# Opening of a bucket-attention kernel: order of the first head's score passes, key bits, casts and moves

## Chip, cores, metric

The kernel runs on one core of a Trainium2 chip. The metric is device time in microseconds (us), the median of three runs. TensorE multiplies matrices, VectorE and GpSimd do elementwise work and reductions, ScalarE does casts and exponentials, and SyncE (SP) issues most of the transfers, each from its own in-order stream of instructions.

## Reference

Attention over 4 batches of 8 heads, 768 positions and 64 dimensions, in which a query sees only the keys of its own bucket. A bucket is the six signs of a projection. The result goes through a mixture of experts with a capacity for each expert.

```python
q_bits = (np.einsum('bhsd,dk->bhsk', q, proj) > 0)      # k_bits the same
q_bucket = np.sum(q_bits * powers, axis=-1)
mask = q_bucket[:, :, :, None] == k_bucket[:, :, None, :]
scores = np.where(mask, scale * np.matmul(q, k.transpose(0, 1, 3, 2)), -1e9)
attn = np.exp(scores - np.max(scores, axis=-1, keepdims=True))
attn = attn / (np.sum(attn, axis=-1, keepdims=True) + 1e-09)
x = np.matmul(attn, v)                                   # then _moe_ref(x, ...)
```

## The kernel before

The 32 heads are worked off in 8 groups of 4 (two pairs of heads, 128 partitions each). For a group, `load` brings q, k and v in float32; `cast` (L130) makes float16 high parts, `sub` (L132) low parts; `bits` (L144) projects q and k and VectorE turns the result into signs `bt` (L145), which ScalarE scales (`bscale`, L146). `dm`, `dm2` and `moves` then send high parts, low parts and signs to the tiles QA, KA, QB, KB by transfers that SP issues. The signs stand in rows 64 to 69 of QA and KA, so that one matmul gives the score and the bucket match.

A head has six score passes (`S_pass`, L240): two matmuls into one of two PSUM tiles, then a maximum on VectorE (L242). `m_rows` (L248, L249) turns three columns of maxima into a row of QA, by three matmuls and ScalarE. `ST` (L258, L259) computes the transposed scores of 128 keys and 384 queries in two matmuls and ScalarE takes the exponential (L260); it needs the row of maxima of its half. `lo` (L263) takes the low part of the probabilities, on GpSimd or, where the lists E0, E1, PAT say so, on VectorE. `AV` (L273 to L275) multiplies with v. `sumv` (L204, L206) and `sumw` (L210 to L214) prepare a correction row of v's sums, which `AV` needs with its last keys.

The steady loop runs over t, 6 steps for each head. Step t issues `ST(t)` for its first half, the score passes planned for t (of head 2 and later, by S and LEAD), the work of half step 2t, the second half of `ST`, `lo` of step t-1, the work of half step 2t+1 and `AV` of step t-4. Each engine takes its instructions in this order.

Ahead of the loop stands the opening, the string OPS. Its words are issued from left to right: a letter is an operation, a digit its argument; words behind the n-th `|` belong to half step n-1 of the loop. Here b are the signs of head 0 (`tbits`, L223 to L225), t, r and l casts and low parts of heads 0 and 1 from a separate early load `XT` (`first`, L67), s a score pass (s0 to s5 head 0, s6 to s11 head 1), m a row of maxima, e a first half of `ST`, B the `bits` of head 1 (L140, from XT) and of pair 1 (L144), a their scaling, D the transfer of head 1's signs (`bdma`, L317), d and f the moves of pair 1 (L152 to L165), c and u its casts and low parts, v and x those of v, C a copy of constant rows (L319), w matmuls that only keep TensorE busy (L76), g an operation of GpSimd that only waits. Before, heads 0 and 1 are handled by the opening, pair 1 (heads 2 and 3) by c, u, d and f, and group 1's casts are planned at half steps 13 to 23 (list P1). Entries 19 to 21 of P1 are the places of group 1's three loads (L62), entry 18 that of `sumv`.

A tile of group 1 takes the place of that of group 0: the load of q waits for the readers of q of pair 1, and the cast of group 1 (L130) writes the tile that the moves of pair 1 read.

Of the kernel before, what the change touches and what calls it, by code (L numbers as in the profile page):

```python
# [17 lines left out]
DR = bass.MemoryType.DRAM  # L18

AP=dict(PAT=[[0, 5], [3]],  # L20
 E0=[3, 5],
 E1=[3, 4],
 X=[2, 2, 5],
 MR=2,
 LEAD=9,
 S=[7, 30],
 DW=[8, 0, 0, 0, 384],
 P1=[13, 13, 14, 15, 17, 21, 23, 21, 16, 27, 21, 26, 23, 24, 33, 32, 3, 4, 50, -6, 3, 13],
 P2=[41, 44, 48, 49, 51, 51, 57, 55, 45, 49, 55, 57, 52, 60, 59, 60, 2, 3, 74, 32, 36, 47],
 P3=[69, 73, 82, 80, 84, 86, 89, 86, 75, 83, 87, 90, 94, 96, 97, 106, 2, 3, 122, 58, 62, 87],  # L30
 P4=[-33, -33, -25, -21, -13, -7, -11, -7, -20, -16, -5, -2, -7, 5, 8, 10, 2, 4, 38, -56, -51, -11],
 L0=[109, 2],

 EA=[(0,0),(0,0),(307,4)],
 SW=9,
 XL={4:[0,3,5],7:[1,4],8:[0,3,5],10:[0,3,5]},
 BS=2,
 MV=[28, 59, 96, 1],
 CL=9,
 WS=-23,  # L40
 SU=15,
 OPS='b0 i3 i2 t0 w2 b1 w3 r0 r2 s0 w4 C1 r1 t1 c1 s1 B0 c0 a0 D0 w2 w1 s4 w5 s2 s3 r3 v2 w5 v0 g0 l0 l1 C0 m0 s5 w3 s6 r5 w2 l3 e0 e1 d0 u0 u1 s7 v1 l2 w0 m1 e2 | s8 | x0 | w0 | x1 s9 | r4 s10 | | | s11 m2 v3 f0 | x3 | | x2 | m3 | | | | | |')
PAT,E0,E1,DW,LEAD=(AP[k] for k in ('PAT','E0','E1','DW','LEAD'))
NB=dict(S=2,T=3,V=1)
HK=385
EMPTY=60000.0
def attention(tc, nc, ctx, qT, kT, vv, proj, wg, x_dram, L, jp, identf, B, late=None, after=None):
    S=768; NG=2*B; NH=8*B; LAG=4
    cp=ctx.enter_context(tc.tile_pool(name="cp",bufs=1))
    dp=ctx.enter_context(tc.tile_pool(name="dp",bufs=2))  # L50
    psS=ctx.enter_context(tc.tile_pool(name="psS",bufs=NB["S"],space=PS))
    psT=ctx.enter_context(tc.tile_pool(name="psT",bufs=NB["T"],space=PS))
    psV=ctx.enter_context(tc.tile_pool(name="psV",bufs=NB["V"],space=PS))
    V=nc.vector; A=nc.scalar; G_=nc.gpsimd; T=nc.tensor; SY=nc.sync
# [3 lines left out]
    def alloc_load(G):  # L58
        LD[G]=(dp.tile([128,2,S],F32,name="qp",bufs=1),dp.tile([128,2,S],F32,name="kp",bufs=1),dp.tile([128,4,6,64],F32,name="vp",bufs=1))
    def load(G,w):  # L60
        if w==0: alloc_load(G)
        SY.dma_start(LD[G][w],(qT,kT,vv)[w][G])  # L62
    alloc_load(0)
    XT=cp.tile([128,4,6,128],F32,name="XT")
    qd,kd=(XT[:,2*i:2*i+2].rearrange("p d c q -> p d (c q)") for i in range(2))
    def first(j,r):
        for t,src in ((qd,qT),(kd,kT)): SY.dma_start(t[r:r+64,j],src[0][64*j:64*j+64,0])  # L67
    first(0,0); first(0,64); first(1,0)
    for w,src in ((0,qT),(1,kT)): SY.dma_start(LD[0][w][:,1],src[0][:,1])
    SY.dma_start(LD[0][2],vv[0])  # L70
    first(1,64)

    wrm=cp.tile([128,512],F16,name="wrm"); V.memset(wrm,0.0)
    wps=psV.tile([128,512],F32,name="psv")
# [8 lines left out]
    pr=cp.tile([128,32],F32,name="pr"); G_.memset(pr,0.0)  # L83
# [41 lines left out]
    def cast(G,w,p,half=None):  # L125
        if (G,'h') not in TMP:
            TMP[G,'h']=[dp.tile([128,2,S],F16,name=n,bufs=1) for n in ("qh","kh")]
            TMP[G,'l']=[dp.tile([128,2,S],F16,name=n,bufs=1) for n in ("ql","kl")]
        if half is None: A.copy(TMP[G,'h'][w][:,p],LD[G][w][:,p])
        else: A.copy(TMP[G,'h'][w][:,p,half*384:half*384+384],LD[G][w][:,p,half*384:half*384+384])  # L130
    def sub(G,w,p,eng=None):
        (eng or G_).tensor_tensor(TMP[G,'l'][w][:,p],LD[G][w][:,p],TMP[G,'h'][w][:,p],op=ALU.subtract)  # L132
    def bits(G,pairs):
        if (G,'b') not in TMP: TMP[G,'b']=dp.tile([128,S],F16,name="bt",bufs=1)
        bt=TMP[G,'b']; r=slice(0,128)
        ps=psS.tile([128,2,512],F32,name="pss")
        for hf in range(2):
            if G==0:
                for w in range(2):
                    T.matmul(ps[32*w:32*w+32,hf,0:384],pr[0:64],(qd,kd)[w][0:64,1,hf*384:hf*384+384],start=True,stop=True,tile_position=(0,32*w))  # L140
            for p in pairs:
                for w in range(2):
                    cg=64*p+32*w
                    T.matmul(ps[cg:cg+32,hf,0:384],pr,LD[G][w][:,p,hf*384:hf*384+384],start=True,stop=True,tile_position=(0,cg))  # L144
        V.tensor_scalar(bt.rearrange("p (z q) -> p z q",z=2),ps[:,:,0:384],0.0,0.5,op0=ALU.is_gt,op1=ALU.subtract)  # L145
# [89 lines left out]
    def S_pass(h,qc):  # L235
        G,j=divmod(h,4); u=G%2
        if qc==0: M6[h]=dp.tile([128,6],F16,name="m6",bufs=3)
        ps=psS.tile([128,2,512],F32,name="pss")
        for hf in range(2):
            T.matmul(ps[:,hf,0:HK],QA[u][:,j,qc*128:qc*128+128],KA[u][:,j,hf*HK:hf*HK+HK],start=True,stop=True)  # L240
            if h==0: warm(DW[1],DW[4])
        V.tensor_reduce(M6[h][:,qc:qc+1],ps[:,:,0:HK],axis=AX.XY,op=ALU.max,negate=True)  # L242
# [72 lines left out]
    def add(n,f,*a): at.setdefault(n,[]).append((f,a))  # L315
    def bdma():
        for w,a in enumerate((QA,KA)): SY.dma_start(a[0][64:70,1,0:S],TMP[0,'b'][32*w:32*w+6])  # L317
    def copies(a):
        for j in (0,2): SY.dma_start(a[1][64:128,j:j+2,0:S],a[0][64:128,2:4,0:S])  # L319
    OPS=dict(i=lambda j: init(j,A.copy),t=top,b=tbits,r=lambda n: rest(n//3,n%3),l=lambda n: rlo(n//2,n%2),  # L320
        c=lambda w: cast(0,w,1),u=lambda w: sub(0,w,1),s=lambda k: S_pass(k//6,k%6),B=lambda n: bits(0,[1]),D=lambda n: bdma(),
        m=lambda n: m_rows(n//2,n%2),d=lambda n: dm(0,[1]),f=lambda n: dm2(0,[1]),v=lambda j: cv(0,j),x=lambda j: sv(0,j,G_),
        e=lambda k: ST(0,k,0),C=lambda n: copies((QA,KA)[n]),w=lambda n: warm(n,DW[4]),a=lambda n: bscale(0),
        g=lambda n: G_.tensor_copy(tick,KA[0][64:65,0,0:1]))
    n=-1; early=[]
# [6 lines left out]
    for G in range(1,NG):  # L332
        p=AP['P1'] if G==1 else AP['P2'] if G==2 else AP['P3'] if G==3 else [48*(G-1)+x for x in AP['P4']]
        st,sg=(AP['P4'] if G>3 else p)[16:18]
        for w in range(3):
            if G==1 or w==2: add(p[19+w],load,G,w)
        for n in range(8): add(p[n],cast,G,n//2%2,n//4,n%2)
        for n in range(4): add(p[8+n],sub,G,n%2,n//2)
        add(p[12],bits,G,[0,1]); add(p[12]+AP['BS'],bscale,G); add(AP['MV'][G-1] if G<4 else 48*(G-1)+AP['MV'][3],moves,G)
        for j in range(4): add(p[15]+st*j,cv,G,j); add(p[15]+st*j+sg,sv,G,j,G_)  # L340
        add(p[18],sumv,G); add(p[18]+AP['SW'],sumw,G)
        if G>1: add(48*(G-1)+AP['CL'],clear,G)

    k=12; done={}; half={}; S_at={}
# [25 lines left out]
    for t in range(6*NH+LAG+6):  # L370
        h,s=divmod(t,6)
        first=(t-LAG)%6==5
# [585 lines left out]
```

## Time and profile before

| | us |
|---|---|
| runs | 714.18, 717.42, 718.44; median 717.42 |
| profiled execution | 718.04, its span 716.3 |
| TensorE busy in the span | 669.1 (93%) |
| VectorE busy | 516.9 (72%) |
| ScalarE busy | 471.4 (66%) |
| GpSimd busy | 517.1 (72%) |

The profile shows one execution; times in it count from the first instruction. TensorE's matmuls overlap in the pipeline, so a busy TensorE is not at its peak. A row's "idle before" names what released the engine. [...]

### The profile page before, as it was taken

How to read it: one execution, taken by the hardware profiler on the slowest of the kernel's cores; microseconds unless marked ns; L12 is line 12 of the kernel's file. 1: busy time of each engine (PE TensorE's matmuls, PEld its weight loads, DVE VectorE, ACT ScalarE, POOL GpSimd, SP SyncE). 2: the span in 40 equal slices, each digit the busy share in tenths (PEclk: the TensorE clock that was granted, in tenths of full speed). 3: DMA queues.
4: the chain of work that ended last, by engine and by line, in shares of the span. 5: the costliest groups of instructions: out<-in, count | busy, mean ns of one | idle time of the engine just before them, and what ended most of it. 6: DMA issues, size and time to landing. Idle time of an engine off the chain costs nothing. (4 is left out here: it accounts for less than half of the span.)

```text
span 716.3 us, 19197 instructions
## 1 busy us (share of the span) xinstructions
PE 669.1 (93%) x7868; PEld 432.4 (60%) x7868; DVE 516.9 (72%) x1126; ACT 471.4 (66%) x887; POOL 517.1 (72%) x456
## 2 busy tenths in 40 slices
PE   8798999999999999999997679999989999999995
PEld 3466666767767777677766455555545465655552
DVE  6858778888888788788975678778777878734120
ACT  7777887777887778777763045665656565666750
POOL 7769979898988979887663237584857475777761
PEclk9989999999999999999998579999999999999998
DMA  7728672725637256440000160727171727272601
GB/s 199 197 75 207 170 195 76 185 69 137 153 105 193 68 139 151 109 102 24 24 24 25 61 220 14 281 61 263 47 277 44 266 61 264 73 266 81 243 29 45
DMA packets 39952, 93.59 MB, mean 131 GB/s; under 512 B 4548, under 2 KB 30520, under 8 KB 37816
## 3 DMA queue, kind: packets, MB, share of 16 engines
q1 hardware_dynamic: 33048, 46.21, 24.6%
q0 software_dynamic: 6816, 46.15, 18.2%
q8 instruction: 62, 1.02, 0.6%
q14 instruction: 26, 0.21, 0.1%
HBM read 59.53 MB, written 12.58 MB: 101 GB/s over the span
## 5 line engine op out<-in xcount | busy, mean ns | idle before, releaser
L263 POOL TENSOR_TENSOR lo<-pt 128x768 f16<-128x768 f32 x139 | 224.3, 1626 | 47.4 <-ACT pt L260 43.0
L260 ACT ACTIVATE pt<-pst 128x384 f32<-128x384 f32 x384 | 181.2, 492 | 73.3 <-PE pst L259 60.9
L242 DVE TENSOR_REDUCE m<-pss 128x1 f16<-128x770 f32 x192 | 181.1, 956 | 35.8 <-PE pss L240 34.6
L258 PE MATMUL pst<-qa,ka 128*128 128x384 f16 x384 | 125.4, 327 | 2.5 <-ACT qa L249 1.3
L259 PE MATMUL pst<-qb,kb 128*128 128x384 f16 x384 | 125.2, 326 | 1.9 <-DMA qb<-ql 1.9
L275 PE MATMUL psv<-vh,lo 128*128 128x65 f16 x1152 | 121.8, 194 | 1.2 <-POOL lo L263 1.1
L274 PE MATMUL psv<-vl,pt 128*128 128x64 f16 x1152 | 122.1, 193 | 0.0
L273 PE MATMUL psv<-vh,pt 128*128 128x65 f16 x1152 | 122.1, 195 | 0.0
L273 PEld LDWEIGHTS <-pt 128*128 128x128 bf16 x1152 | 107.2, 98 | 11.1 <-issue 3.5
L274 PEld LDWEIGHTS <-pt 128*128 128x128 bf16 x1152 | 106.3, 99 | 8.2 <-issue 0.3
L275 PEld LDWEIGHTS <-lo 128*128 128x128 f16 x1152 | 106.3, 98 | 1.6 <-POOL lo L263 1.6
L785 POOL TENSOR_TENSOR wl<-wf,wh 128x512 f16<-128x512 f32 x76 | 87.2, 1173 | 22.0 <-ACT wf L776 21.6
L240 PE MATMUL pss<-ka,qa 128*128 128x385 f16 x384 | 94.6, 329 | 1.4 <-DVE m L242 0.6
L767 ACT ACTIVATE wh<-wf 128x1024 f16<-128x1024 f32 x64 | 67.0, 1052 | 34.9 <-PE psa L735 20.9
L263 DVE TENSOR_TENSOR lo<-pt 128x768 f16<-128x768 f32 x53 | 73.4, 1385 | 1.6 <-ACT pt L260 1.0
L828 PEld LDWEIGHTS <-wh 128*128 128x128 f16 x512 | 48.3, 98 | 35.5 <-issue 5.4
L840 PEld LDWEIGHTS <-hh 128*128 128x128 f16 x384 | 35.9, 97 | 39.6 <-issue 2.0
L776 ACT ACTIVATE wf<-wf 128x1024 f32<-128x1024 f32 x55 | 58.1, 1057 | 1.0
L831 DVE SCALAR_TENSOR_TENSOR hl<-px,hh 128x384 f16<-128x384 f32 x64 | 34.9, 552 | 31.2 <-ACT hh L830 30.7
L843 ACT ACTIVATE o<-po 128x512 f32<-128x512 f32 x24 | 14.3, 595 | 64.9 <-PE po L840 63.8
L828 PE MATMUL px<-xh,wh 128*128 128x384 f16 x256 | 53.9, 327 | 3.2 <-ACT xh L815 2.4
L240 PEld LDWEIGHTS <-qa 128*128 128x128 f16 x384 | 37.2, 97 | 27.8 <-issue 1.5
(271 smaller groups left out, 1328.0 us busy)
## 6 DMA issues: line engine op xcount, KB each, us to landing
vp<-in_vv_dram SPq DMA_DIRECT2D x8, 768.0 KB
x_dram<-X SPq DMA_DIRECT2D x16, 384.0 KB
qp<-in_qT_dram SPq DMA_DIRECT2D x7, 768.0 KB
kp<-in_kT_dram SPq DMA_DIRECT2D x7, 768.0 KB
qa<-qh SPq DMA_DIRECT2D x14, 192.0 KB
ka<-kh SPq DMA_DIRECT2D x14, 192.0 KB
qb<-qh SPq DMA_DIRECT2D x14, 192.0 KB
kb<-kh SPq DMA_DIRECT2D x14, 192.0 KB
```

What stands on the lines that cost most here:

```text
L240: T.matmul(ps[:,hf,0:HK],QA[u][:,j,qc*128:qc*128+128],KA[u][:,j,hf*HK:hf*HK+HK],start=True,stop=True)
L242: V.tensor_reduce(M6[h][:,qc:qc+1],ps[:,:,0:HK],axis=AX.XY,op=ALU.max,negate=True)
L258: T.matmul(ps[:,0:384],KA[u][:,j,kr],QA[u][:,j,r],start=True,stop=False)
L259: T.matmul(ps[:,0:384],KB[u][:,j,kr],QB[u][:,j,r],start=False,stop=True)
L260: A.activation(PT[h,kc][0][:,r],ps[:,0:384],AF.Exp,scale=0.125)
L263: eng.tensor_tensor(l,p,p.bitcast(BF)[:,1::2],op=ALU.subtract)
L273: T.matmul(av[:,c,:],ph[:,r],VH[u][:,j,kc,:],start=(kc==0 and c==0),stop=False,skip_group_check=True)
L274: T.matmul(av[:,c,0:64],ph[:,r],VL[u][:,j,kc,:],start=False,stop=False,skip_group_check=True)
L275: T.matmul(av[:,c,:],l[:,r],VH[u][:,j,kc,:],start=False,stop=False,skip_group_check=True)
L767: s.nc.scalar.mul(h[:,r],f[:,r],WSC)
L785: for _ in range(n): s.nc.gpsimd.tensor_tensor(*s.pend.pop(0)[1],op=ALU.subtract)
L828: T.matmul(p[:,0:384],a[:,o:o+128],b[:,d],start=n==0,stop=n==11)
```

## The change

The opening is reordered. Head 0's six score passes stand ahead of the bits of head 1 and pair 1 (B0), with three first halves of `ST` (e0 to e2) and the first row of maxima (m0); the score passes of head 1 (s6 to s11) move into the loop, half steps 4 to 11. `C0` moves ahead of `D0`, `f0` from half step 7 to 9. Group 1's loads of q and k (L0, L1) move from half steps -6 and 3 of the planned list into the opening, ahead of the moves d0. `first(1,64)` goes ahead of the loads of pair 1 and of v, and B0 uses all 128 rows of XT and `pr`. The low parts of pair 1 go from GpSimd to VectorE. Head 0's low parts on VectorE are those of steps 0 and 5 instead of 3 and 5, head 1's those of 1, 3 and 4 instead of 3 and 4. S delays the passes of head 2 and a few behind it: the first stands at step 5 instead of 3. `sumv` comes one to three half steps earlier, `sumw` four half steps behind it instead of nine.

```diff
--- before.py
+++ after.py
@@ -18,28 +18,28 @@
 DR = bass.MemoryType.DRAM
 
 AP=dict(PAT=[[0, 5], [3]],
- E0=[3, 5],
- E1=[3, 4],
+ E0=[0, 5],
+ E1=[1, 3, 4],
  X=[2, 2, 5],
  MR=2,
  LEAD=9,
- S=[7, 30],
+ S=[7, 7],
  DW=[8, 0, 0, 0, 384],
- P1=[13, 13, 14, 15, 17, 21, 23, 21, 16, 27, 21, 26, 23, 24, 33, 32, 3, 4, 50, -6, 3, 13],
- P2=[41, 44, 48, 49, 51, 51, 57, 55, 45, 49, 55, 57, 52, 60, 59, 60, 2, 3, 74, 32, 36, 47],
- P3=[69, 73, 82, 80, 84, 86, 89, 86, 75, 83, 87, 90, 94, 96, 97, 106, 2, 3, 122, 58, 62, 87],
- P4=[-33, -33, -25, -21, -13, -7, -11, -7, -20, -16, -5, -2, -7, 5, 8, 10, 2, 4, 38, -56, -51, -11],
+ P1=[13, 13, 14, 15, 17, 21, 23, 21, 16, 27, 21, 26, 23, 24, 33, 32, 3, 4, 49, -6, 3, 13],
+ P2=[41, 44, 48, 49, 51, 51, 57, 55, 45, 49, 55, 57, 52, 60, 59, 60, 2, 3, 72, 32, 36, 47],
+ P3=[69, 73, 82, 80, 84, 86, 89, 86, 75, 83, 87, 90, 94, 96, 97, 106, 2, 3, 121, 58, 62, 87],
+ P4=[-33, -33, -25, -21, -13, -7, -11, -7, -20, -16, -5, -2, -7, 5, 8, 10, 2, 4, 35, -56, -51, -11],
  L0=[109, 2],
 
  EA=[(0,0),(0,0),(307,4)],
- SW=9,
+ SW=4,
  XL={4:[0,3,5],7:[1,4],8:[0,3,5],10:[0,3,5]},
  BS=2,
  MV=[28, 59, 96, 1],
  CL=9,
  WS=-23,
  SU=15,
- OPS='b0 i3 i2 t0 w2 b1 w3 r0 r2 s0 w4 C1 r1 t1 c1 s1 B0 c0 a0 D0 w2 w1 s4 w5 s2 s3 r3 v2 w5 v0 g0 l0 l1 C0 m0 s5 w3 s6 r5 w2 l3 e0 e1 d0 u0 u1 s7 v1 l2 w0 m1 e2 | s8 | x0 | w0 | x1 s9 | r4 s10 | | | s11 m2 v3 f0 | x3 | | x2 | m3 | | | | | |')
+ OPS='b0 i3 i2 t0 w2 b1 w3 r0 r2 s0 w2 s1 C1 C0 r1 t1 w4 s2 r3 w3 s3 r5 g0 l0 l1 m0 s4 e0 s5 e1 e2 l3 B0 c1 m1 c0 a0 D0 u0 u1 L0 L1 l2 v0 e3 d0 | x0 | v1 | x1 | v2 | s6 v3 | x2 s7 | r4 s8 | x3 | s9 | m2 f0 | s10 | s11 | m3 | | |')
 PAT,E0,E1,DW,LEAD=(AP[k] for k in ('PAT','E0','E1','DW','LEAD'))
 NB=dict(S=2,T=3,V=1)
 HK=385
@@ -65,10 +65,9 @@
     qd,kd=(XT[:,2*i:2*i+2].rearrange("p d c q -> p d (c q)") for i in range(2))
     def first(j,r):
         for t,src in ((qd,qT),(kd,kT)): SY.dma_start(t[r:r+64,j],src[0][64*j:64*j+64,0])
-    first(0,0); first(0,64); first(1,0)
+    first(0,0); first(0,64); first(1,0); first(1,64)
     for w,src in ((0,qT),(1,kT)): SY.dma_start(LD[0][w][:,1],src[0][:,1])
     SY.dma_start(LD[0][2],vv[0])
-    first(1,64)
 
     wrm=cp.tile([128,512],F16,name="wrm"); V.memset(wrm,0.0)
     wps=psV.tile([128,512],F32,name="psv")
@@ -137,7 +136,7 @@
         for hf in range(2):
             if G==0:
                 for w in range(2):
-                    T.matmul(ps[32*w:32*w+32,hf,0:384],pr[0:64],(qd,kd)[w][0:64,1,hf*384:hf*384+384],start=True,stop=True,tile_position=(0,32*w))
+                    T.matmul(ps[32*w:32*w+32,hf,0:384],pr,(qd,kd)[w][:,1,hf*384:hf*384+384],start=True,stop=True,tile_position=(0,32*w))
             for p in pairs:
                 for w in range(2):
                     cg=64*p+32*w
@@ -318,7 +317,7 @@
     def copies(a):
         for j in (0,2): SY.dma_start(a[1][64:128,j:j+2,0:S],a[0][64:128,2:4,0:S])
     OPS=dict(i=lambda j: init(j,A.copy),t=top,b=tbits,r=lambda n: rest(n//3,n%3),l=lambda n: rlo(n//2,n%2),
-        c=lambda w: cast(0,w,1),u=lambda w: sub(0,w,1),s=lambda k: S_pass(k//6,k%6),B=lambda n: bits(0,[1]),D=lambda n: bdma(),
+        c=lambda w: cast(0,w,1),L=lambda w: load(1,w),u=lambda w: sub(0,w,1,V),s=lambda k: S_pass(k//6,k%6),B=lambda n: bits(0,[1]),D=lambda n: bdma(),
         m=lambda n: m_rows(n//2,n%2),d=lambda n: dm(0,[1]),f=lambda n: dm2(0,[1]),v=lambda j: cv(0,j),x=lambda j: sv(0,j,G_),
         e=lambda k: ST(0,k,0),C=lambda n: copies((QA,KA)[n]),w=lambda n: warm(n,DW[4]),a=lambda n: bscale(0),
         g=lambda n: G_.tensor_copy(tick,KA[0][64:65,0,0:1]))
@@ -333,7 +332,7 @@
         p=AP['P1'] if G==1 else AP['P2'] if G==2 else AP['P3'] if G==3 else [48*(G-1)+x for x in AP['P4']]
         st,sg=(AP['P4'] if G>3 else p)[16:18]
         for w in range(3):
-            if G==1 or w==2: add(p[19+w],load,G,w)
+            if w==2: add(p[19+w],load,G,w)
         for n in range(8): add(p[n],cast,G,n//2%2,n//4,n%2)
         for n in range(4): add(p[8+n],sub,G,n%2,n//2)
         add(p[12],bits,G,[0,1]); add(p[12]+AP['BS'],bscale,G); add(AP['MV'][G-1] if G<4 else 48*(G-1)+AP['MV'][3],moves,G)
```

## Rows read from the trace of the kernel before

**Rows 1.** Table of stretches: from:to, length, busy us (instructions) by engine, clock, DMA share, GB/s
```profile
22.35:32.90 10.55, 9.64 (x105) 6.13 (x105) 9.81 (x10) 8.22 (x17) 9.71 (x9) 1.00 0.70 206
32.90:36.20 3.30, 0.01 (x2) 0.02 (x2) 2.03 (x2) 1.62 (x4) 3.15 (x3) 0.83 0.87 234
36.20:42.60 6.40, 6.40 (x81) 4.73 (x81) 1.46 (x2) 4.31 (x10) 2.44 (x2) 0.55 0.14 57
65.00:79.00 14.00, 12.14 (x186) 7.89 (x185) 10.71 (x13) 9.52 (x22) 11.80 (x9) 1.00 0.62 177
200.00:240.00 40.00, 39.66 (x638) 28.70 (x637) 33.75 (x45) 31.66 (x69) 35.83 (x39) 1.00 0.47 117
24.90:34.50 9.60, 7.34 (x93) 4.94 (x92) 9.57 (x9) 5.74 (x12) 9.60 (x8) 1.00 0.88 249
```
**Rows 2.** Waits of TensorE, us in total, times, longest: 0:42.6, then 42.6:390
```profile
PE pst L204 <- ACT qa L249: 3.3, 1, 3.3
...
PE pst L259 <- DMA qb<-ql: 1.9, 1, 1.9
```
**Rows 3.** TensorE's timeline in the opening: start us, duration us, operation, [idle before <-releaser]
```profile
11.14 0.83 PE L140 MATMUL pss<-XT,pr 64*32 64x384 f32 x4
...
14.21 0.66 PE L76 MATMUL psv<-wrm 128*128 128x384 f16 x3
...
24.72 0.49 PE L240 MATMUL pss<-ka,qa 128*128 128x385 f16 x2 [0.25 <-DMA ka<-bt]
```
**Rows 4.** TensorE's timeline, one step of the loop at full clock
```profile
26.93 0.19 PE L273 MATMUL psv<-vh,pt 128*128 128x65 f16 x1
...
27.48 0.33 PE L258 MATMUL pst<-qa,ka 128*128 128x384 f16 x1
...
27.80 0.49 PE L240 MATMUL pss<-ka,qa 128*128 128x385 f16 x2
28.14 0.32 PE L258 MATMUL pst<-qa,ka 128*128 128x384 f16 x1
```
**Rows 5.** TensorE's timeline, the bits of group 1: first matmul, and the first behind them
```profile
46.36 0.51 PE L144 MATMUL pss<-qp,pr 128*32 128x384 f32 x1
...
47.79 0.21 PE L273 MATMUL psv<-vh,pt 128*128 128x65 f16 x1
```
**Rows 6.** VectorE's timeline
```profile
10.12 1.94 DVE L242 TENSOR_REDUCE m<-pss 128x1 f16<-128x770 f32 x2 [0.67 <-PE pss L240]
14.35 0.96 DVE L145 TENSOR_SCALAR bt<-pss 128x768 f16<-128x768 f32 x1 [2.29 <-PE pss L144]
...
23.53 4.43 DVE L242 TENSOR_REDUCE m<-pss 128x1 f16<-128x770 f32 x5 [0.71 <-PE pss L240]
27.99 2.23 DVE L263 TENSOR_TENSOR lo<-pt 128x768 f16<-128x768 f32 x1
...
44.49 0.95 DVE L263 TENSOR_TENSOR lo<-pt 128x768 f16<-128x768 f32 x1
```
**Rows 7.** ScalarE's timeline
```profile
15.34 0.84 ACT L146 ACTIVATE bt<-bt 128x768 f16<-128x768 f16 x1 [3.08 <-DVE bt L145]
...
26.11 0.66 ACT L249 ACTIVATE qa<-pst,mbi,msc 32x384 f16<-32x384 f32 x1
...
34.53 0.93 ACT L130 CAST qh<-qp 128x384 f16<-128x384 f32 x2 [3.62 <-DMA kb<-kl]
...
49.92 0.83 ACT L146 ACTIVATE bt<-bt 128x768 f16<-128x768 f16 x1
```
**Rows 8.** SP's timeline of issues: start us, issue us, transfer
```profile
16.21 0.86 SPq L317 DMA_DIRECT2D qa<-bt  x1
17.12 0.72 SPq L317 DMA_DIRECT2D ka<-bt  x1
...
22.68 0.71 SPq L158 DMA_DIRECT2D ka<-bt  x1
...
24.91 0.37 SPq L62 DMA_DIRECT2D qp<-in_qT_dram  x1
```

## The prediction

> **What bounds the kernel now.** I read the table of stretches first, then the waits of TensorE, then the timelines of the five engines over the opening. Between 200 and 240 us TensorE is busy 39.66 of 40 us at full clock [rows 1], and from 42.6 to 390 us it has one wait over 1 us, 1.9 us for the transfer `qb<-ql` before the first transposed score of head 4 [rows 2]. So TensorE sets the pace of the attention. Work that reaches the end of head 0 earlier moves everything behind it, unless a transfer holds it back. [...] The reader should see the cause on ScalarE: the first cast of group 1 (L130) starts at 34.53 us after 3.62 us of waiting, put down to `kb<-kl`, one of the eight moves for heads 2 and 3 [rows 7]. Those moves stand in SP's queue behind the two loads of group 1 issued from 24.91 us [rows 8]. That queue is full: 249 GB/s, DMA share 0.88, from 24.9 to 34.5 us [rows 1]. Everything behind the cast on ScalarE, exponentials and row maxima, waits with it, so TensorE does too.
>
> **What that costs.** 3.3 us idle, and 6.4 us of work at 0.55 that full clock would do in 6.4 x 0.55 = 3.5 us: 2.9 us. Together 6.2 us is what a perfect opening could win back there.
>
> **The change, part by part.** Prices first. Per TensorE step: a transposed pair 27.80 - 27.48 = 0.32 us, a score pass 0.34 us, one `AV` 0.55 us (26.93 to 27.48) [rows 4]. A maximum on VectorE comes every 4.43/5 = 0.89 us [rows 6]. Signs to `bt` 0.96 us [rows 6], scaling on ScalarE 0.84 us, row of maxima 0.66 us [rows 7], a cast of 768 columns 0.8 us (an estimate: just under the scaling, which has as many columns).
>
> (1) *Six score passes ahead of the key bits.* Pass 0 is not moved: its maximum starts at 10.12 us [rows 6]. Six maxima in a row end at 10.12 + 6 x 0.89 = 15.5 us. The third ends at 12.8, so the first row of maxima is written by about 13.9 (0.4 us for the matmuls, 0.66 for ScalarE), and the first transposed score starts near 14.0 us. Three of them and pass 5 take 1.3 us, so the key bits start at 15.3 us instead of 11.14 [rows 3].
>
> (2) *Key bits with 128 rows.* The bits of head 1 used 64 rows of the array, those of pair 1 use 128, and the timeline shows them one after the other: 11.14 to 14.21 us, 3.07 us [rows 3]. Group 1's bits are four column groups of 128 rows, run beside each other, and as many matmuls of as many columns take 47.79 - 46.36 = 1.43 us [rows 5]. With all operands at 128 rows the opening's bits have that same form, so I take 1.43 us; the bounds are 1.43 and 3.07. The bits end at 16.75.
>
> (3) *What then waits.* Signs to 17.8, row of maxima 17.1 to 17.8, cast of q to 18.6, scaling to 19.4. The two transfers of head 1's signs are issued 19.4 and 20.3 (before: 16.21 and 17.12 [rows 8]). From issue to use, the sign transfer issued at 22.68 took until 24.72 [rows 3, 8], 2.0 us. So head 1's first score pass can start at 22.3 us. TensorE has by then only the fourth transposed score and two second halves left, and is done at 18.5. It takes its instructions in order and that pass stands at the third step of the loop, so behind it wait all second halves. **New wait 1: 22.3 - 18.5 = 3.8 us** (3.4 if the transfer takes 1.6).
>
> (4) *Low parts of pair 1 on VectorE.* Alone, a low part takes 0.95 us there, beside a busy GpSimd 2.23 [rows 6]. Without these two, the order gives GpSimd little to do just then, so I take 0.95 each: 18.6 to 20.5, before the signs of head 1 are out, so hidden; at 2.23 the second ends at 23.1 and delays the load of k by about 2 us. The extra low part of head 1 on VectorE costs the same, 0.95 to 2.23, and there VectorE is loaded.
>
> (5) *Loads of group 1 ahead of the moves for heads 2 and 3.* They go out at 21.05 and 21.55, 3.9 us earlier than before. But now the four moves and four sign transfers of pair 1 stand behind them. Two loads of 768 KB and four moves of 96 KB are 1.97 MB; at the 249 GB/s of rows 1 that is 7.9 us: 29.0, with the signs 29.2. Bounds: by issue alone 27.3, at the 234 GB/s of 32.9 to 36.2 us 29.7. Head 2's first score pass stands at step 5 and needs them. From 22.3 TensorE has four score passes paced by maxima, five transposed halves and one `AV`, until 26.5. **New wait 2: 29.2 - 26.5 = 2.7 us** (0.8 to 3.2).
>
> (6) *The old wait.* The eight moves of `dm2` follow those of d0: sixteen transfers at some 0.7 us of issue each [rows 8], from 21.9 us, are issued by 33.1 and the last land near 35, about as before. ScalarE, held by waits 1 and 2, reaches the cast only about then: its own wait is gone or under 1 us. From 29.2 on three maxima (2.7), the row (1.1), `AV` and three passes (1.6) bring TensorE to the sum of v (L204) near 35.1 us, against 36.20.
>
> (7) *From there.* The stretch that took 6.4 us takes 3.5 at full clock; the extra low part on VectorE ahead of the correction of v adds 0.9 to 2.2 (I take 1.3: GpSimd is busy beside it for a part only). 35.1 + 3.5 + 1.3 = 39.9 to 40.7 (with the row of maxima now falling there), against 42.6: 2.4 us ahead, taking 40.2.
>
> (8) *Up to the bits of group 1.* Head 2's passes are two fewer by then, since they start at step 5 instead of 3, so one more maximum (0.89) and what is left of (7) must pass VectorE before the bits: 1.0 us lost. The scaling of group 1's bits (49.92, [rows 7]) comes 1.4 us earlier. All sign transfers, loads and moves of group 1 follow it in SP's order, so the 1.9 us wait of rows 2 moves along, neither shrinking nor growing.
>
> (9) *Sums of v one to three half steps earlier, corrections four instead of nine behind.* Around them TensorE shows no wait in 200 to 240 us [rows 1]: nothing, bounds 0.5 us either way; what covers it is TensorE's own queue.
>
> Sum: -1.4 us against the profiled execution's 718.04 us (span 716.3 and 1.7 around it): 716.6. That execution is 0.6 us above the median of 717.42, so a median would be 716.0. I say 716.4.
>
> **A rule that speaks against it.** After 3.3 us without matmuls the clock stood at 0.55 over the next stretch [rows 1]; after the 1.9 us of rows 2 it did not fall (1.00 from 65 to 79 us, [rows 1]). Wait 1 is of the first kind. [...]
>
> **Rivals.** *Clock falls behind wait 2* (or stays low through it): 2.9 us by the price above, less 0.6 that waits on VectorE cover: 718.7, slower than the profiled execution. It decides when wait 2 is as long as the old 3.3, or when the clock has not risen by 29 us; against it, 2.7 is shorter. *Moves are not held by the loads*: wait 2 shrinks to 0.8, 1.9 gained: 714.5; for it, the bound by issue, against it, the full queue. *The bits are not shortened*: 3.07 us delay everything behind by 1.6: 718.0. *The gain is kept whole*: the 6.2 us and the 1.6 of the bits, off the median: 709.6; against it, the last moves cannot land before 33, so the cast cannot start over 1.5 us earlier. *Several microseconds slower*: a new wait on VectorE at each group, over 725; nothing in rows shows it.
>
> **How the numbers follow.** Forecast 0.56, clock 0.17, moves not held 0.12, bits not shortened 0.06, gain whole 0.05, far slower 0.04. Within 1% is 710.2 to 724.6, about what measurement can tell from no change; only the last two leave it: faster 0.05, same 0.90, slower 0.05. The range goes from the third case, less the 1.7 by which the runs before differ downwards among themselves at the least (717.42 to 714.18 is 3.2), 712.8, to the clock case with 2.23 us low parts, 720.2. The forecast's own range is 714.5 to 718.5.
>
> **What would show it.** Right: key bits of 1.4 us near 15 us; a gap of 3 to 4 us on TensorE before 22 us put down to `ka<-bt`; one of 2 to 3 us before 29; the first cast of group 1 near 35 with little wait; group 1's scaling near 48.5. Wrong: no gap at step 3, or the cast before 33 (faster); or a clock below 1.00 after 30 us (slower).

## The result, and the profile after

The changed kernel takes 720.24 us (median of 13 runs, 716.36 to 722.93), the kernel before, beside it, 715.81 (13 runs, 713.59 to 718.83): ratio 1.0059 (95% interval 1.0035 to 1.0082; intervals stand in square brackets from here on), some 4.4 us slower. 716.4 was forecast, 1 us faster than before. The profiled execution of the changed kernel took 722.02 us (span 720.2), against 718.04.

Lines after the change lie one lower. First the timelines of the profiled execution: start us, duration us, engine, line, operation, [idle before <-releaser]. TensorE to the end of head 0:

```profile
5.05 2.72 PE L222 MATMUL pst<-XT,prt 64*6 64x384 f32 x4 [0.26 <-DMA prt<-in_proj_dram]
...
12.30 0.80 PE L239 MATMUL pss<-ka,qa 128*128 128x385 f16 x2
...
15.47 0.85 PE L239 MATMUL pss<-ka,qa 128*128 128x385 f16 x2
...
16.95 0.49 PE L239 MATMUL pss<-ka,qa 128*128 128x385 f16 x2
...
19.81 0.52 PE L139 MATMUL pss<-XT,pr 128*32 128x384 f32 x2
...
26.77 0.57 PE L239 MATMUL pss<-ka,qa 128*128 128x385 f16 x2 [3.63 <-DMA ka<-bt]
...
34.65 0.82 PE L239 MATMUL pss<-ka,qa 128*128 128x385 f16 x4 [2.39 <-DMA ka<-bt]
```

The two waits of the prediction are there, 3.63 and 2.39 us, both for the signs `ka<-bt` (forecast 3.8 and 2.7). But they end 4.5 and 5.4 us later than forecast, and the first rows show why: the signs of head 0 take 2.72 us for four matmuls, and the first score passes 0.80 to 0.85 us for two, until one at 16.95 takes 0.49. That is TensorE at about half its speed, the lower level, until some 16 us. The granted clock, a share of full speed, reads 1.00 there all the same (from 4.5 to 9.5 us and from 12 to 16), so at the start only the durations tell. In the execution of before that was profiled, the same code up to the first pass ran at the upper level, 1.45 us for the same four matmuls:

```profile
5.18 1.45 PE L223 MATMUL pst<-XT,prt 64*6 64x384 f32 x4 [0.53 <-DMA prt<-in_proj_dram]
...
9.59 0.49 PE L240 MATMUL pss<-ka,qa 128*128 128x385 f16 x2 [0.55 <-DVE ka L225]
```

ScalarE and VectorE:

```profile
39.95 0.92 ACT L129 CAST qh<-qp 128x384 f16<-128x384 f32 x2
...
54.70 0.84 ACT L145 ACTIVATE bt<-bt 128x768 f16<-128x768 f16 x1
...
71.25 0.51 ACT L129 CAST qh<-qp 128x384 f16<-128x384 f32 x1 [1.70 <-DMA kp<-in_kT_dram]
```
```profile
13.15 0.96 DVE L241 TENSOR_REDUCE m<-pss 128x1 f16<-128x770 f32 x1 [0.99 <-PE pss L239]
...
23.17 0.96 DVE L131 TENSOR_TENSOR ql<-qp,qh 128x768 f16<-128x768 f32 x1 [0.81 <-ACT qh L128]
24.04 0.95 DVE L131 TENSOR_TENSOR kl<-kp,kh 128x768 f16<-128x768 f32 x1
...
47.18 2.13 DVE L262 TENSOR_TENSOR lo<-pt 128x768 f16<-128x768 f32 x1
49.23 2.68 DVE L241 TENSOR_REDUCE m<-pss 128x1 f16<-128x770 f32 x3
```

The first cast of group 1 has no wait any more (3.62 before [rows 7]). In place of the low part of 0.95 us at 44.49 [rows 6] stands one of 2.13, and three maxima queue behind it.

The waits of TensorE from 56 to 90 us (total, times, longest) and the stretch at heads 2 and 3 (columns as in [rows 1]):

```profile
PE pst L258 <- DMA qb<-ql: 2.6, 1, 2.6
PE pst L257 <- ACT pt L259: 1.2, 1, 1.2
```
```profile
76.00:82.00 6.00, 3.83 (x40) 2.29 (x41) 0.96 (x1) 2.82 (x7) 2.70 (x2) 0.72 0.31 116
```

The 1.9 us wait of [rows 2] is 2.6 here, with another of 1.2 ahead of it, and the granted clock over this stretch is 0.72 on average; before, it was 1.00 from 65 to 79 us [rows 1].

For what follows I read points from the timeline of each execution: start of the first score pass, first cast of group 1, scaling of group 1's bits, and the reciprocal (VectorE) with which heads 0, 2, 3 and 31 are divided. "Issue" is the time on SP from the issue of the last sign transfer of group 1 to that of the last of its four low-part moves, for which the transposed scores of head 4 wait. All in us, one execution each.

| kernel | first pass | cast | scaling | issue | head 0 | head 2 | head 3 | head 31 | time |
|---|---|---|---|---|---|---|---|---|---|
| before | 9.6 | 34.5 | 49.9 | 7.8 | 42.9 | 65.0 | 79.0 | 387.6 | 718.04 |
| before, 12 matmuls at the start (b_w12) | 9.7 | 33.7 | 47.3 | 7.8 | 40.3 | 62.4 | 76.2 | 385.1 | 715.80 |
| before, later sums of v (b_sums) | 12.5 | 37.3 | 50.9 | 7.5 | 43.9 | 66.0 | 79.3 | 386.3 | 715.30 |
| before, none (b_cold) | 12.5 | 42.2 | 56.7 | 7.6 | 49.7 | 71.7 | 85.4 | 395.3 | 723.54 |
| after | 12.3 | 40.0 | 54.7 | 9.7 | 45.6 | 70.1 | 88.0 | 394.7 | 722.02 |
| after, again (after_8) | 12.5 | 41.1 | 55.9 | 9.7 | 46.8 | 71.3 | 87.7 | 395.6 | 724.80 |
| after, old sums of v (a_sums_back) | 9.5 | 35.2 | 50.0 | 9.4 | 40.9 | 65.4 | 80.6 | 389.6 | 717.38 |
| after, low parts back (a_lo_back) | 9.7 | 37.5 | 52.3 | 9.6 | 43.2 | 67.7 | 85.5 | 393.2 | 721.99 |
| after, none (a_cold) | 12.4 | 40.0 | 54.7 | 8.4 | 45.7 | 70.2 | 84.8 | 391.8 | 720.99 |
| after, 16 (a_warm) | 11.9 | 39.5 | 54.3 | 7.8 | 45.2 | 69.7 | 82.6 | 390.7 | 717.67 |
| after, 12 matmuls (a_w12_2) | 9.8 | 35.7 | 50.5 | 7.8 | 41.4 | 65.9 | 79.2 | 386.1 | 714.85 |

From head 31 to the end it is 327 to 331 us, so some us of a difference at head 31 can be gone or added at the end; where is open.

### The profile page after: what moved, and what is told of

Read it like the earlier page. It is cut to its first block, busy times and chain, and to the rows that moved or that the text cites. A ratio compares the mean times of both kernels' runs of the same rounds, so it can differ in the third digit from the quotient of the medians.

```text
span 720.2 us, 19169 instructions
## 1 busy us (share of the span) xinstructions
PE 670.2 (93%) x7855; PEld 431.6 (60%) x7855; DVE 507.5 (70%) x1128; ACT 471.9 (66%) x887; POOL 511.6 (71%) x454
## 5 line engine op out<-in xcount | busy, mean ns | idle before, releaser
L241 DVE TENSOR_REDUCE m<-pss 128x1 f16<-128x770 f32 x192 | 181.9, 957 | 47.3 <-PE pss L239 46.1
L239 PE MATMUL pss<-ka,qa 128*128 128x385 f16 x384 | 96.2, 335 | 8.2 <-DMA ka<-bt 6.0
L262 DVE TENSOR_TENSOR lo<-pt 128x768 f16<-128x768 f32 x53 | 62.6, 1182 | 1.7 <-ACT pt L259 1.4
```

The lines of the kernel that those rows point to most:

```text
L262: eng.tensor_tensor(l,p,p.bitcast(BF)[:,1::2],op=ALU.subtract)
```

## The experiments

**The late part, alone and undone.** Two kernels: before with the new places of `sumv` and `sumw`, and after with the old ones.

```diff
- P1=[... 50, -6, 3, 13], ... SW=9      (P2: 74, P3: 122, P4: 38)
+ P1=[... 49, -6, 3, 13], ... SW=4      (P2: 72, P3: 121, P4: 35)
```


> The kernel before with the change's last part alone: sums of v one to three half steps earlier, corrections four half steps behind them instead of nine. Theory of the opening (all of the measured +4.4 us comes from the opening): no difference, within 1 us of before. Rival, the late part costs it: +3 to +5 us over before, with new waits of TensorE at L204 or L210 behind 70 us. This is also a second look at the opening of before: if the granted clock rises as late as in the changed kernel's profile (16.8 us instead of 4.4), that is a matter of the execution and not of the change.

> The changed kernel with the old places of the sums of v and of their corrections. Theory of the opening: as the changed kernel, +4 us over before, the waits for the signs of head 1 (3.6 us) and of head 2 (2.4 us) both there again. Rival, the late part: within 1 us of before. The clock of its opening is open: if it rises near 5 us, head 0 should end near 43 us instead of 45.6.

b_sums 715.46, ratio to before 0.9993 [0.9959, 1.0026]; a_sums_back 719.79, 1.0066 [1.0035, 1.0096]. Alone, the late part costs nothing that can be told; without it the loss is there. So the loss lies in the rest of the change, the opening and the plan for heads 0 to 3. The execution of a_sums_back happens to begin early (first pass 9.5), and there the opening goes as forecast: wait 1 of 3.61 us from 18.6, wait 2 of 2.44 from 27.5, cast 35.2, head 0 at 40.9, 2.0 us ahead of before (TensorE, then the cast on ScalarE):

```profile
15.26 0.52 PE L139 MATMUL pss<-XT,pr 128*32 128x384 f32 x2
...
22.21 0.81 PE L239 MATMUL pss<-ka,qa 128*128 128x385 f16 x2 [3.61 <-DMA ka<-bt]
...
29.92 0.82 PE L239 MATMUL pss<-ka,qa 128*128 128x385 f16 x4 [2.44 <-DMA ka<-bt]
```
```profile
35.22 0.92 ACT L129 CAST qh<-qp 128x384 f16<-128x384 f32 x2
```

At head 3 it is 1.6 us behind before.

**Key bits with 128 rows, alone.** Before with:

```diff
-    first(0,0); first(0,64); first(1,0)
+    first(0,0); first(0,64); first(1,0); first(1,64)
- T.matmul(ps[...],pr[0:64],(qd,kd)[w][0:64,1,...],...)
+ T.matmul(ps[...],pr,(qd,kd)[w][:,1,...],...)
```


> The kernel before with the key bits of the opening at 128 rows alone (second halves of head 1's early load ahead of the other loads). Theory: the bits take 1.4 us instead of 3.07, the signs of head 1 and the moves of pair 1 are issued 1.6 us earlier, and the first cast of group 1, which waits for them, starts near 32.9 instead of 34.5: 1 to 2 us faster than before. Rival, the queue of transfers is the bound: loads and moves land when they did, the cast stays at 34.5, no difference.

718.14, 1.0009 [0.9982, 1.0036]: no difference in the runs. The bits took 2.3 us there (11.13 to 13.46) and not 1.4; in the profiled execution, the fastest of the runs, head 31 is at 385.4.

**Moves ahead of the loads.** After with `d0` ahead of `L0 L1`:

```diff
- D0 u0 u1 L0 L1 l2 v0 e3 d0 |
+ D0 u0 u1 d0 L0 L1 l2 v0 e3 |
```


> The changed kernel with the moves of pair 1 (d0) ahead of group 1's two loads in SP's order. Theory, the second new wait is a cost: the 2.4 us wait of head 2's first score pass goes, and the time falls by 1.5 to 2.4 us against the changed kernel (+2 to +3 over before). Rival, the loads are the bound: they land 5 us later, near 36 us, the eight later moves behind them near 40 as before, the first cast of group 1 waits instead, and the time stays at +4 over before.

717.89, 1.0025 [0.9996, 1.0055]. Wait 2 is gone; in its place TensorE waits 1.8 us for the exponentials:

```profile
PE pss L239 <- DMA ka<-bt: 3.6, 1, 3.6
PE pst L257 <- ACT pt L259: 1.8, 1, 1.8
```

The cast stays at 35.3, now behind a wait of 2.57 us for `qb<-qh`, and head 0 at 41.0 (40.9 in a_sums_back, which began as early). So wait 2 is the loads ahead of the moves, and in these two executions taking it away gains nothing at the end of head 0. In the runs it is 1.9 us below a_sums_back on the same chip; whether by this edit is not shown.

**No matmuls at the start.** Both kernels with `DW=[8, ...]` set to `DW=[0, ...]`, so that both begin at the lower level (2.72 us for the four matmuls of head 0's signs in both profiles, as in after).

> The kernel before without the eight matmuls that run first, so that the clock cannot be up when the signs of head 0 are computed (of the six profiles so far it was up by 5.1 us in four and only at 13.9 or 16.8 us in two). Theory, the state of the clock at the start decides how much the change costs: before loses little by a cold opening, 0 to +1.5 us, since it waits for the first cast of group 1 anyway (profile of the same opening with the clock up at 13.9 us: end of attention at 386.3 us against 387.6). Rival, the start does not matter to the comparison: before and changed kernel lose the same by a cold opening.

> The changed kernel without the eight first matmuls. Theory: the six passes stand ahead of the key bits and of everything that hangs on them, so the 2.8 us of a cold start and the slower matmuls behind it come out at the signs, the first cast of group 1 and the end: +6 to +8 us over before. Rival: the same loss as in before, so +4 to +5 over before as the changed kernel itself.

b_cold 723.57, 1.0040 [1.0007, 1.0073]; a_cold 720.68, 1.0012 [0.9983, 1.0041] (another chip, before at 719.33). Both expectations missed: the old order lost 4.2 us (0 to 1.5 expected), the changed one 1.3 (6 to 8). Forced to a late start, the changed order is the faster of the two, though its 720.68 is what the plain changed kernel took. It is no equal start: in the profiles the score passes of a_cold are at the upper level from 17.0 us (0.49 us for two matmuls), while one of b_cold at 21.8 us still takes 0.85.

**Low parts of the probabilities back.** After with `E0=[3,5]` and `E1=[3,4]`.

> The changed kernel with the old places of the low parts on VectorE for heads 0 and 1 (steps 3 and 5, and 3 and 4). Theory, VectorE is late ahead of the bits of group 1 (a 1.70 us wait of TensorE for a maximum): one low part of 1 to 2 us less there takes that wait to under 0.8 us, and group 1's scaling comes 1 us earlier: 0.5 to 1.5 us faster than the changed kernel. Rival, the maxima themselves are late (they start at step 5): the wait stays at 1.5 to 1.9 us, no difference.

719.66, 0.9989 [0.9955, 1.0022]. The 1.70 us wait of TensorE for the maximum ahead of group 1's bits was unchanged:

```profile
47.81 0.49 PE L239 MATMUL pss<-ka,qa 128*128 128x385 f16 x2 [1.70 <-DVE m L241]
```

The reason is in the code: line 390 (391 before) gives the name E1 to another list, and the loop reads the name only when it runs.

```
390: E1=[-12,-4,-3,2,6,8,10,13,16,19,22,25,28,31,34,37,43,50]
```

In 0 to 5 that has only step 2. Both kernels have exactly one low part of head 1 on VectorE, so the change of E1, given above as part of the change, has no effect, and this run undid E0 alone. Its execution began early (9.7) and still had wait 2 at 3.60 us and head 31 at 393.2: a late start is not the only way to a slow execution.

**Load of k of group 1 later, in before.**

```diff
- P1=[..., 50, -6, 3, 13]
+ P1=[..., 50, -6, 8, 13]
```


> The kernel before with the load of k of group 1 planned at half step 8 instead of 3, so behind the eight moves of pair 1 in SP's order instead of ahead of them. Theory, those moves behind 1.5 MB of loads are what holds the first cast of group 1: it starts near 32.4 us instead of 34.5, the cast of k near 35, TensorE's wait shrinks from 3.3 to about 1.2 us, the clock does not fall: 2 to 4 us faster than before. Rival, the queue's throughput is the bound and the wait moves to the cast of k: within 1 us of before.

716.37, 0.9951 [0.9914, 0.9989], 3 us faster. The wait of 3.3 us [rows 2] is gone from TensorE's list, and the clock does not fall:

```profile
36.00:44.00 8.00, 6.82 (x108) 4.43 (x106) 7.10 (x6) 6.71 (x15) 8.00 (x6) 1.00 0.89 270
```

**Sixteen matmuls at the start; head 1 without a low part on VectorE; a mixed version.** b_warm and a_warm: `DW=[16, ...]`. a_warm_lo2: a_warm, and

```diff
- E0 if hh<1 else E1 if hh<2 else ...
+ E0 if hh<1 else () if hh<2 else ...
```

The mixed version, b_best, is before with the later k, the 128-row bits, the new sums of v and `DW=[12, ...]`.

> The kernel before with sixteen instead of eight matmuls in the first burst that only keeps TensorE busy (DW[0] 8 to 16). Theory: whether the granted clock is up near 4.5 us or only at 14 to 24 us is a matter of the execution, and it moves the whole opening; the longer burst (some 1.2 to 6.4 us instead of 1.2 to 4.7) brings the clock up in nearly every execution, at a price of about 1.2 us for the first signs. Then the times should lie closer together than those of before, the clock should be up by 8 us in the profile, first pass near 10.8, first scaling near 20, and the median within 1.5 us of before. Rival, the start decides nothing: 1.2 us slower than before with the same spread.

> The changed kernel with the same sixteen matmuls at the start. Theory: with the same start the change costs about 2 us (end of head 31 in the profile 389.6 against 387.6 with a warm start in both), so 1.5 to 2.5 us slower than the kernel before with the same sixteen matmuls. Rival A, the start has nothing to do with it: some 4.4 us slower than it, as in the plain comparison. Rival B, the changed order wins whenever the start is equal, as with a cold start (2.9 us faster): faster than it.

> The changed kernel, sixteen matmuls at the start, and head 1 without any low part on VectorE: the one of step 2 goes to GpSimd. (The lists E1 of the two kernels play no part: the name is given another list further down in the file, so that both kernels have this one low part there, at 44.49 us for 0.95 us before and at 47.18 us for 2.13 us, beside GpSimd, after.) Theory: the wait of 1.70 us of the score pass ahead of group 1's bits is that low part, 2.13 us ahead of a maximum. Without it the wait falls below 0.5 us, group 1's scaling comes about 9 us behind the division of head 0 has been reached less 1.5 (7.6 instead of 9.1 us behind it), the transfers of group 1 with it, and the time is 1 to 1.5 us below the changed kernel with sixteen matmuls. Rival: GpSimd, busy there, is later by 1.47 us, so that AV or the low part of q waits for it and the time is the same or longer.

> The kernel before with those edits that did not hurt by themselves: group 1's load of k at half step 8 instead of 3, the key bits with 128 rows (and the fourth early load ahead of the loads of pair 1), the sums of v and their corrections at the changed places, and twelve matmuls at the start. Theory: no wait of 3.3 us and no fall of the clock in 32 to 43 us (3 us), bits shorter by 1.6 us of which up to 2.2 us was seen at the end of head 31, first signs 0.8 us later: 3 to 4.5 us below before, ratio 0.994 to 0.996, attention in the profile done by 385. Rival: the gains overlap, since both free the same place (the transfers behind which ScalarE's first cast of group 1 waits): 2 to 3 us, no more than with the later load alone.

b_warm 717.44, 1.0010 [0.9981, 1.0039]; a_warm 717.02, 0.9995 [0.9968, 1.0021]; a_warm_lo2 717.05, 1.0013 [0.9984, 1.0041]; b_best 711.67, **0.9945 [0.9912, 0.9977]**. With sixteen matmuls the change makes no difference that can be told (a_warm to b_warm, worked out from their runs, 0.9994 [0.9975, 1.0016]), neither the 2 us of my theory nor the 4.4 or the gain of the rivals. In a_warm_lo2 the scaling comes 7.5 us behind the division of head 0 (42.7 and 50.2) instead of 9.1, and the wait of 1.70 us is 0.44, so the low part was that wait (VectorE):

```profile
43.37 1.82 DVE L241 TENSOR_REDUCE m<-pss 128x1 f16<-128x770 f32 x2
45.63 1.83 DVE L241 TENSOR_REDUCE m<-pss 128x1 f16<-128x770 f32 x2 [0.44 <-PE pss L239]
48.23 0.96 DVE L144 TENSOR_SCALAR bt<-pss 128x768 f16<-128x768 f32 x1 [0.78 <-PE pss L143]
```

But the time is the same: TensorE waits 1.47 us for `qb<-ql` and 1.18 for ScalarE at heads 2 and 3. b_best beats before, and lies 5.4 us below a_warm on the same chip.

**Twelve matmuls, and group 2's load of k behind the moves.** b_w12 and a_w12: `DW=[12, ...]`. a_w12_k2 is a_w12, and b_best2 is b_best, each with this in `moves`:

```diff
- if G==1: qa(); ka(); signs(); nxt(0); qb(); kb(); nxt(1)
+ if G==1: qa(); ka(); signs(); nxt(0); qb(); kb()
  ... (the low parts)
+ if G==1: nxt(1)
```


> The kernel before with twelve instead of eight matmuls in the first burst. Theory: sixteen brought the clock up in every execution seen, but cost 1.9 us of start (first pass at 11.5 instead of 9.6 us); twelve, as in the mixed kernel, start the first pass near 9.8 with the clock up near 4.5. So 0 to 1.5 us faster than with eight: 0.998 to 1.000. Rival, some executions stay at the lower level until 14 to 24 us as with eight: 1.000, spread as before.

> The changed kernel with twelve matmuls at the start. Theory: with the clock up by 5 us in every execution, end of head 0 near 41 (31.4 us behind the first pass, as in the four executions of this order with one fall of the clock), end of head 31 near 389.5: 716 to 717.5, so 0 to 2 us slower than the kernel before with twelve. Rival A, the change costs 4.4 us whatever the start: 720. Rival B, with an equal start there is no difference, as with sixteen (717.0 against 717.4): within 0.7 us of the kernel before with twelve.

> The changed kernel with twelve matmuls at the start and group 2's load of k issued behind all moves of group 1 instead of ahead of the moves of the low parts. Theory: what sets the end of heads 2 and 3 are the transfers of group 1 behind its scaling. In the two executions above 720 us TensorE waited 2.3 and 2.6 us for qb<-ql and 1.2 to 1.3 us for ScalarE, the clock fell at 76 to 78 us, and from the division of head 2 to that of head 3 it took 17.9 us (12.9 to 15.3 in the others). Without 768 KB ahead of the low parts (3.1 us at 249 GB/s) the wait for qb<-ql falls below 0.5 us, head 2 to head 3 takes 13 to 13.7, and the time is 1.5 to 2.5 us below the same kernel without this edit. Rival: the wait is for the issue of the low parts, or the later k of group 2 makes ScalarE wait by as much: same time.

> The mixed version that was 4.4 us faster than before (later load of k of group 1, key bits with 128 rows, sums of v at the changed places, twelve matmuls) with group 2's load of k behind all moves of group 1. Theory: its wait of 1.02 us for qb<-ql goes: 710.5 to 711.5 where the kernel before stands at 716, ratio 0.992 to 0.994. Rival: the cast of group 2's k is late by 3 us and ScalarE waits: 712 or more.

b_w12 718.20, 0.9992 [0.9961, 1.0023]; a_w12 717.06, 0.9987 [0.9956, 1.0018]; a_w12_k2 718.86, 1.0004 [0.9978, 1.0030]; b_best2 713.73, **0.9931 [0.9900, 0.9962]** (before at 718.78). Again no loss: rival B is nearest. In a_w12_k2 no wait for `qb<-ql` is left and head 2 to head 3 takes 13.0 us, as expected, but it is not faster than a_w12 (1.8 us slower, ratio worked out from the runs 1.0025 [0.9999, 1.0049]), whose wait was only 0.9 us. So moving that load takes the wait away, but it was small here anyway. The same edit in the kernel with eight matmuls, where the wait is long, was not run. The mixed version wins again with it; that the edit adds anything is not shown.

**Eight against twelve on one chip.** after_8 is the changed kernel as it is, a_w12_2 the one with `DW=[12, ...]`.

> The changed kernel as it is, with eight matmuls at the start, beside the same with twelve on one chip. Theory: the loss of the plain comparison is the start; the end of head 0 lies 31.4 to 33.3 us behind the first score pass wherever that is (9.5 to 12.4 us), since both new waits hang on TensorE's own earlier work, so that executions whose clock comes up late end late. So 719 to 721 where the one with twelve takes 717, a median 0.3 to 0.6% apart, with the wider spread here. Rival, the differences between the runs so far are those of the chips: both within 0.15% of each other.

> The changed kernel with twelve matmuls at the start, as before, on one chip with the one with eight. Theory: 0.3 to 0.6% below it, 716.5 to 717.5, first score pass near 10 us, clock up by 5 us, end of head 0 31.4 to 33.3 us behind the first pass. Rival: no difference from the one with eight.

after_8 721.06 (715.65 to 725.13), 1.0033 [0.9999, 1.0068]; a_w12_2 717.20 (714.85 to 720.91), 0.9996 [0.9972, 1.0019]. The changed kernel is slower than before again, by 2.7 us, though this interval just reaches no change. Four matmuls that compute nothing are worth 3.9 us to it, the ratio of the two worked out from their runs 1.0054 [1.0016, 1.0101]. First the stretches 4.5 to 9.5, 12 to 20 and 36 to 40 us of after_8, then of a_w12_2:

```profile
4.50:9.50 5.00, 4.59 (x9) 0.72 (x9) 1.46 (x3) 4.88 (x7) 2.94 (x17) 1.00 1.05 220
12.00:20.00 8.00, 7.34 (x36) 3.48 (x38) 5.63 (x7) 2.02 (x4) 6.59 (x5) 1.00 0.69 167
...
36.00:40.00 4.00, 3.08 (x27) 2.10 (x27) 2.88 (x5) 1.49 (x3) 0.00 (x0) 0.57 0.76 160
```
```profile
4.50:9.50 5.00, 4.79 (x18) 1.11 (x16) 2.98 (x6) 4.88 (x7) 2.96 (x17) 1.00 1.05 218
12.00:20.00 8.00, 5.73 (x43) 2.46 (x41) 5.80 (x8) 6.00 (x10) 4.50 (x3) 1.00 0.67 163
...
36.00:40.00 4.00, 3.78 (x61) 2.48 (x59) 1.93 (x2) 3.90 (x11) 3.80 (x3) 1.00 0.71 229
```

From 4.5 to 9.5 us TensorE is about as busy, but does half as many instructions in after_8, 9 against 18. Then the waits of over 0.8 us in the first two groups of heads that differ or move, in after_8 and in a_w12_2 (TensorE's timeline):

```profile
26.79 0.80 PE L239 MATMUL pss<-ka,qa 128*128 128x385 f16 x2 [3.61 <-DMA ka<-bt]
...
34.69 0.82 PE L239 MATMUL pss<-ka,qa 128*128 128x385 f16 x4 [2.65 <-DMA ka<-bt]
...
73.58 0.32 PE L257 MATMUL pst<-qa,ka 128*128 128x384 f16 x1 [1.37 <-ACT pt L259]
...
79.37 0.32 PE L258 MATMUL pst<-qb,kb 128*128 128x384 f16 x1 [2.38 <-DMA vp<-in_vv_dram]
...
117.56 0.20 PE L274 MATMUL psv<-vh,lo 128*128 128x65 f16 x1 [1.65 <-POOL lo L262]
```
```profile
22.48 0.80 PE L239 MATMUL pss<-ka,qa 128*128 128x385 f16 x2 [3.61 <-DMA ka<-bt]
...
30.39 0.82 PE L239 MATMUL pss<-ka,qa 128*128 128x385 f16 x4 [1.32 <-DMA ka<-kh]
...
70.86 0.32 PE L258 MATMUL pst<-qb,kb 128*128 128x384 f16 x1 [0.84 <-DMA qb<-ql]
```

Wait 1 is the same 3.61 us wherever the first pass stands, 4.3 us later here (3.61 to 3.63 us in all eleven executions of the changed order): it hangs on TensorE's own bits and cannot absorb a late start. The 2.7 us at the first pass are 4.3 at the end of both waits and 5.4 at head 0 (the clock falls behind wait 2, 0.57) and at head 2. Then they are 8.5 at head 3 and 9.5 at head 31. That second step has a place of its own, SP's issues of group 1's last moves, in the profiled execution of after and then in a_w12_2: last signs, two moves of the high part of q, last move of the low part.

```profile
60.65 0.66 SPq L173 DMA_DIRECT2D ka<-bt  x1
...
61.84 3.04 SPq L177 DMA_DIRECT2D qb<-qh  x2
...
70.39 0.61 SPq L187 DMA_DIRECT2D qb<-ql  x1
```
```profile
56.40 0.66 SPq L173 DMA_DIRECT2D ka<-bt  x1
...
57.59 2.47 SPq L177 DMA_DIRECT2D qb<-qh  x2
...
64.19 0.78 SPq L187 DMA_DIRECT2D qb<-ql  x1
```

In after, SP waits 1.6 us between two of the four low-part moves, by the profile for `qp<-in_qT_dram`, the load of q of group 2; in a_w12_2 it does not. This issue time goes with the time from head 2 to head 3 in all twenty executions: where it is 6.8 to 7.8 us, that takes 12.8 to 14.0; where it is 8.4 to 10.0, 14.6 to 17.9. It does not go with the start: in the changed order it was long in all five executions with eight matmuls, three of them early, and in a_cold, short in the three with twelve, and once each with sixteen. In the old order it was long in one execution of nine.

## Why the prediction was wrong, point by point

Two steps failed. Step 1 took the start of the first maximum, 10.12 us, over from one execution as if it were given, with no range; in the profiled execution after it was 13.15. Step 8 kept 1.4 us of the lead and let the wait behind the scaling move along unchanged; the runs show that the scaling loses 2.1 us and not 1.0, and that from head 2 to head 3 it then takes up to 17.9 us, against 14.0 before. Against the forecast (1.4 us ahead of before behind the scaling), the profiled execution is 2.7 us late at the first pass, 5.4 at head 0, 10.5 at head 3 and 8.5 at head 31.

**The start.** Of nine executions with eight matmuls at the start (before's order and after's, single parts moved) four began late, at 12.3 to 12.5 us: two of four in the old order, two of five in the changed one. Of nine with twelve or sixteen none stayed at the lower level behind the first matmuls (1.45 to 1.48 us for the four matmuls of the signs, against 2.72 in after, after_8 and b_sums). The old order does not hide a late start either: b_sums began 2.8 us later than b_w12 and was 3.6 us behind at head 0, 3.1 at head 3 and 1.2 at head 31; b_cold, also 2.8 later, was 9.4 behind at head 0 and 10.2 at head 31. In the runs, twelve instead of eight matmuls make no difference to before (0.9992) and take 3.9 us from after. The rivals had no such case. In number the clock rival (718.7) came nearest; the clock did fall behind wait 2 in four of the eleven executions of the changed order (in after_8 to 0.57 from 36 to 40 us), not in the profiled one (1.00 from 34 to 42 us).

**What is shown and what is not.** Shown is that four more matmuls at the start take the loss away. By which way is open. The late start is one: after and after_8 reach head 0 4.2 and 5.4 us behind a_w12_2. The moves for heads 4 to 7, whose issue heads 2 and 3 pay for, are the other: a_lo_back began early and was slow with them, and a_warm reaches head 2 within 0.5 us of after, has short issues, and ends 4.35 us earlier. Why twelve matmuls should shorten those issues is not known. Each kernel has a trace of one run only, so how often it starts late is open too; and with no burst at all the old order is the slower one.

**Given a clock that is up from the start**, the change does little: 717.06 against 718.20 with twelve (ratio worked out from the runs 0.9984 [0.9960, 1.0017]), 717.02 against 717.44 with sixteen. The forecast of -1.4 us cannot be told from that.

**Steps 1 to 6**, in a_sums_back, apart from the start: right within about 1 us. The bits began at 15.26 (15.3) and took 1.43 us also in after (19.81 to 21.24); wait 1 was 3.61 us from 18.6 (3.8 from 18.5), wait 2 2.44 from 27.5 (2.7 from 26.5), the cast at 35.2 (35), with little wait, the sum of v at 36.1 (35.1 in step 6, whose own terms add up to 34.6). The low parts of pair 1 took 0.96 and 0.95 us. In a_w12_2 wait 2 is 1.32 us only, since the clock stayed at its lower level longer behind wait 1; the stretch 24 to 28 us there:

```profile
24.00:28.00 4.00, 4.00 (x17) 2.09 (x16) 2.94 (x4) 2.45 (x5) 4.00 (x5) 0.50 1.00 342
```

In both, head 0 ends 31.3 to 31.6 us behind the first pass, so wait 2 does hide the fall of the clock behind wait 1. That the clock falls behind wait 1, as it did behind the 3.3 us of [rows 2], is borne out: in the stretch behind it the clock stood at 0.50 in all eleven executions (in after from 27.5 to 30 us, in a_w12_2 from 24 to 28). For shorter waits it is open: the clock fell behind 2.65 us in after_8 (0.57 from 36 to 40 us) and 2.59 in b_bits128 (0.82 from 36 to 44), and not behind 2.65 in b_sums (1.00 from 36 to 44), 2.44 in a_sums_back (1.00 from 28 to 36) or 2.38 in b_w12 (1.00 from 32 to 40).

**Step 7**: head 0 at 40.9 and 41.4 instead of 40.2. One term of it, 1.3 us for an extra low part of head 1, belongs to work that does not exist (E1), so the rest was 2 us too short. And the 6.2 us that stood to be won is the price of one execution: b_w12 has the same start as before, a wait of 2.38 us in place of 3.30, no fall of the clock, and reaches head 0 at 40.3 with the old order.

**Step 8** failed by its size: from the division of head 0 to the scaling it takes 9.1 us instead of 7.0, a loss of 2.1 and not 1.0. It is the low part on VectorE that was there before too. It now starts while GpSimd is in a low part of its own (from 47.02 to 48.49 us in after) and takes 2.13 us; before, it started ahead of GpSimd's (44.49 against 44.95) and took 0.95 (GpSimd in before, then in after):

```profile
44.95 1.81 POOL L263 TENSOR_TENSOR lo<-pt 128x768 f16<-128x768 f32 x1 [5.75 <-ACT pt L260]
```
```profile
47.02 1.47 POOL L262 TENSOR_TENSOR lo<-pt 128x768 f16<-128x768 f32 x1 [2.52 <-ACT pt L259]
```

The lead of 2.0 us in a_sums_back is gone by then, the scaling at 50.0 against 49.9, and the sign transfers behind it go out when they did before. That the wait for `qb<-ql` "moves along, neither shrinking nor growing", was wrong: in the changed order it is between less than 0.8 and 2.6 us, by the execution, long where the issue time above is long, and behind the 2.6 of the profiled one the clock fell (0.56 from 78 to 80 us). **Step 9** was right within what the runs can tell (0.9993 [0.9959, 1.0026]).

## What to carry to other kernels

Before a change of a microsecond or two is summed against one execution, ask what in that execution differs from run to run: here the level of TensorE's clock at the start, which only the durations show (2.72 against 1.45 us for the same four matmuls, at a granted clock of 1.00 in both). A wait that hangs on an engine's own earlier work, as wait 1 does, moves along with it and takes up nothing of a late start (3.61 to 3.63 us, for a first pass between 9.5 and 12.5 us). Follow a difference point by point to the end, and do not put all of it down to the first place where it shows: here some of it arose again at heads 2 and 3. And look up where a name is given its value last: one part of this change was a list that nothing reads.

## What was not expected of the hardware

The same code up to the first score pass took 9.5 to 9.7 us or 12.3 to 12.5. With eight matmuls ahead of it, the level of TensorE's clock varies from execution to execution (1.45 or 2.72 us for the four matmuls of the signs); its price alone is not measured. Four more matmuls at the start were worth 0.5% (721.06 against 717.20), with whatever else they changed, nearly as much as the whole difference measured.

A low part on VectorE took 0.95 us, or 2.1 to 2.2 where GpSimd was already in one of its own; nothing in its instruction differs. Where VectorE's started first (44.49 in before), GpSimd's of 44.95 took 1.81 us instead of the 1.47 that it takes in after.
